# Fused attention and gated MLP: three edits to the opening, to slot 1 and to SyncE's queue

## The chip, the cores and the metric

The kernel runs on one NeuronCore of a Trainium2 chip. The metric is device time in microseconds (us), the median of several runs. A profile shows one further execution: its span runs from the first to the last instruction, and the execution's own time is a little longer than that.

## What is computed

The reference, cut to what matters (B = 8 batches, H = 8 heads, S = 576 rows, D = 64, 32 packed queries p per head; w_in is 512 x 2048, w_out 2048 x 512; all float32):

```python
def sm_attn(qq, kk, vv):
    s = scale * np.matmul(qq, kk.transpose(0, 1, 3, 2))
    a = np.exp(s - np.max(s, axis=-1, keepdims=True))
    a = a / (np.sum(a, axis=-1, keepdims=True) + 1e-09)
    return np.matmul(a, vv)

p_packed = sm_attn(p, k, v)
out = sm_attn(q, p_packed, p_packed)
x = out.transpose(0, 2, 1, 3).reshape(B * S, H * D)
h = x @ w_in
return (h * np.cos(h)) @ w_out
```

## The kernel before

The order of all work is written out by hand; nothing reorders it within an engine. The batches are worked off in slots. For batch b:

- k, q and v are cast to bf16 while POOL's DMA loads them (load, L92). kT and qT are their transposes. For the first batches TensorE makes them (pe_T, L103); later a DMA transpose does, issued in SyncE's queue (xbar, L96).
- s1 (L142): scores of the packed queries against kT, then their exponentials a1 on ScalarE. a1 is transposed to a1T, by TensorE (a1_pe, L163) or by a DMA transpose in SyncE's queue (a1_xbar, L158). pp (L173) multiplies a1T by v, pp_T transposes the result.
- ppw (L195) multiplies it by w_in, in four pieces of 512 columns; the result is PPW. s2, sums2 and normalise (L221 to L244) make the second softmax, a2n, from qT.
- The slot proper, slot(b) (L468): 16 steps, one for each 128 of the 2048 hidden columns. Each step runs h_mm (L248): four matmuls of PPW and a2n into a psA buffer, the cosine on ScalarE (L258), the product h * cos(h) on VectorE into gT (L261). There are three psA buffers in all, used in turn by all of these stages.
- Between these, TensorE is given output matmuls of the batch before (out_gen, L331; w_out, line L339): fill(n) issues the next n of them. 16 make a chunk of 128 rows, which ScalarE or VectorE copies to an osb buffer (there are four) and SyncE stores. In slot(s, hooks, keep, heavy) the output matmuls that are left, less keep, are spread over the 16 steps in proportion to the weights 1 + heavy[step]; a hook (other work given for a step) runs ahead of the step's output matmuls, but at a step that stands in heavy half of them go ahead of it.

Batch 0 has no earlier outputs to fill with, so the opening has matmuls of zeros in TensorE's order (warm, L373): 7 ahead of pack_p(0, 1), the transposes of the first packed queries, and 9 between it and pe_T of k0. Their operand wz is zeroed by VectorE (L388). Others stand later in the opening and aren't touched. q0's transposes, s2 and normalise follow, then 16 steps of h_one (L274) that alternate ScalarE and VectorE.

Slot 1 has as a hook at step 4 h_rest(0) (L286): the last 64 rows of batch 0 for all 16 column groups at once: 32 small matmuls into one psA buffer, one cosine over 1024 columns (L295), one product (L297, to joint). At step 5 comes a piece of ppw, at step 6 pack_p(2, 4), at steps 8 to 10 the transposes of k2.

In slots 3 to 7 (the loop at L542) SyncE's queue is given, in each slot that has a next one: xbar of q of the next batch (L551), a1_xbar of the next batch (L556), and, where there is one, xbar of k of the batch after (L559). SyncE's queue is in order, and the output stores stand in it as well. POOL waits for that k (the copy to gate, L560) before it issues the loads of v, q and k for later batches (L573).

Of the kernel before, what the change touches and what calls it, by code (L numbers as in the profile page):

```python
# [8 lines left out]
FP32 = mybir.dt.float32  # L9
# [6 lines left out]
def kernel(  # L16
# [10 lines left out]
    nc = tc.nc  # L27
# [12 lines left out]
    const = ctx.enter_context(tc.tile_pool(name="const", bufs=1))  # L40
# [22 lines left out]
    V, ACT, G = nc.vector, nc.scalar, nc.gpsimd  # L63
# [32 lines left out]
    def xbar(n, b):  # L96
        t = xT[n, b] = att_pool.tile([128, H * 3, TP], BF16, name=n + "T", tag=n + "T", bufs=2 if n == "k" else 1)
        nc.sync.dma_start_transpose(out=t, in_=bf[n, b].rearrange("p h x -> p (h x)"))
# [4 lines left out]
    def pe_T(n, b, engs=(V, V, V), groups=(0, 1, 2), own=None):  # L103
        if 0 in groups:
            xT[n, b] = att_pool.tile([128, H * 3, TP], BF16, name=n + "T", tag=n + "T", bufs=2 if n == "k" else 1)
        t = xT[n, b]
        flat = bf[n, b].rearrange("p h x -> p (h x)")
        for i in groups:
            ps = own(BF16) if own else psa(BF16)[:, 0, :]
            for j in range(8):  # L110
                o = 8 * i + j
                nc.tensor.transpose(ps[:, j * TP:(j + 1) * TP], flat[:, o * 128:(o + 1) * 128],  # L112
                                    ident[0:TP, 0:TP])
            copy(engs[i], t[:, 8 * i:8 * i + 8].rearrange("p a x -> p (a x)"),
                 ps[:, 0:8 * TP])

    def bank(dt=FP32):
        return O.tile([128, 512 if dt == FP32 else 1024], dt, name="ot", tag="ot")

    def pack_p(b0, b1, flat=None):  # L120
        ng = 2 * (b1 - b0)
        if flat is None:
            flat = psa(BF16).rearrange("p a x -> p (a x)")
        for g in range(ng):
            nc.tensor.transpose(flat[:, g * 128:(g + 1) * 128],
                                p_bf[:, 2 * b0 + g].rearrange("p t d -> p (t d)"), ident)
        V.tensor_copy(out=P2[:, b0:b1].rearrange("p b h n -> p (b h n)"), in_=flat[:, 0:ng * 128])
# [14 lines left out]
    def s1(b):  # L142
        ps = scores(lambda r, h, e: P2[r, b, h, :], xT["k", b])
        sm = small.tile([128, 2], FP32, name="sums1")
        for y in range(2):
            ACT.activation(  # L146
                out=a1[b % 2][:, y, :, 0:TP].rearrange("p (e m) x -> p e m x", e=2),
                in_=ps[y][:, :, 0:HS].rearrange("p e (m x) -> p e m x", m=3),
                func=AF.Exp, scale=scale, accum_out=sm[:, y:y + 1])
        sums1[b] = sm  # L150

    def recips(b):
        r1[b] = small.tile([128, 2], FP32, name="r1")
        rs1[b] = small.tile([128, 2], FP32, name="rs1")
        V.reciprocal(r1[b], sums1[b])
        V.tensor_scalar(out=rs1[b], in0=r1[b], scalar1=scale, scalar2=None, op0=ALU.mult)

    def a1_xbar(b):  # L158
        t = a1T[b] = att_pool.tile([128, 2, C, 128], BF16, name="a1T", tag="a1T")
        nc.sync.dma_start_transpose(out=t.rearrange("p a c x -> p (a c) x"),  # L160
                                    in_=a1[b % 2].rearrange("p a c x -> p (a c x)"))
# [33 lines left out]
    def ppw(b, n, eng=None, own=False, later=False, cuts=((0, 512),)):  # L195
        if b not in PPW:
            PPW[b] = ppw_pool.tile([128, 2, DF], BF16, name="PPW", tag="PPW")
        two = isinstance(eng, tuple)
        if own:
            ps = [bank(), bank()]  # L200
        else:
            t = psa()
            ps = [t[:, 0, :], t[:, 1, :]]
        for x in range(4):
            for y in range(2):
                r = slice(64 * y, 64 * y + 64)
                nc.tensor.matmul(ps[y][32 * x:32 * x + 32, :], ppT[b % 2][r, 0, x, :],  # L207
                                 w_in_bf[r, x, n * 512:(n + 1) * 512], start=True, stop=True)

        def evacuate(cuts=cuts):  # L210
            if own or two:
                for a, z in cuts:
                    for y in range(2):
                        copy(eng[y] if two else eng, PPW[b][:, y, n * 512 + a:n * 512 + z], ps[y][:, a:z])
            else:
                copy(eng or (V, ACT)[n % 2], PPW[b][:, :, n * 512:(n + 1) * 512], t)
        if later:
            return [lambda c=c: evacuate((c,)) for c in cuts]
        evacuate()

    def s2(b):  # L221
        a2u[b] = att_pool.tile([128, 2, S], BF16, name="a2u", tag="a2u")
        ps = scores(lambda r, h, e: ppT[b % 2][r, (h + e) % 2, h // 2, :], xT["q", b])
        for y in range(2):
            ACT.activation(out=a2u[b][:, y].rearrange("p (e x) -> p e x", e=2),  # L225
                           in_=ps[y][:, :, 0:HS], func=AF.Exp, scale=rs1[b][:, y:y + 1])

    def sums2(b, y):
        if b not in lns:
            lns[b] = att_pool.tile([128, 2, S], FP32, name="lns", tag="lns")  # L230
        ps = psa()
        for e in range(2):
            nc.tensor.matmul(ps[:, e, 0:HS], ones_blk, a2u[b][:, y, e * HS:(e + 1) * HS],  # L233
                             start=True, stop=True)
        ACT.activation(out=lns[b][:, y].rearrange("p (e x) -> p e x", e=2),  # L235
                       in_=ps[:, :, 0:HS], func=AF.Ln)

    def normalise(b):
        a2n[b] = a2n_pool.tile([128, 2, S], BF16, name="a2n", tag="a2n")
        for y in range(2):  # L240
            ACT.activation(out=lns[b][:, y], in_=lns[b][:, y], func=AF.Exp, scale=-1.0)  # L241
        for y in range(2):
            V.scalar_tensor_tensor(out=a2n[b][:, y], in0=a2u[b][:, y], scalar=r1[b][:, y:y + 1],  # L243
                                   in1=lns[b][:, y], op0=ALU.mult, op1=ALU.mult)  # L244
# [105 lines left out]
    def set_filler(b):  # L350
        fill(1000)
        filler[0] = out_gen(b)
        filler[1] = 16 * n_chunks(b)

    def fill(n):
        while n > 0 and filler[1] > 0:
            next(filler[0])
            filler[1] -= 1
            n -= 1
# [9 lines left out]
    def dup_p(a, b, eng):  # L369
        for t in range(2):  # L370
            eng.tensor_copy(out=p_bf[:, a:b, t, :], in_=p_raw[:, a:b, :])

    def warm(n, wps=None):  # L373
        wps = bank() if wps is None else wps
        for _ in range(n):
            nc.tensor.matmul(wps, wz[:, 0:128], wz, start=True, stop=True)  # L376

    nc.sync.dma_start(out=p_raw[:, 0:2, :], in_=p_rows[:, 0:2, :])
    load("k", 0)
# [6 lines left out]
        load_w_in(n)  # L386
    wz = const.tile([128, 512], BF16, name="wz")
    V.memset(wz, 0.0)  # L388
    ACT.preload_act_table_set(EXP_SET)
    V.memset(ones_blk, 0.0)  # L390
    for j in range(4):
        V.memset(ones_blk[j * 32:(j + 1) * 32, j * 32:(j + 1) * 32], 1.0)
    for t in a1:
        V.memset(t[:, :, :, TP:128], 0.0)

    warm(7)
    dup_p(0, 2, V)
    pack_p(0, 1)
    warm(9)
    pe_T("k", 0, (V, ACT, V))  # L400
    s1(0)
    load_w_in(3)
# [83 lines left out]
    def tk(n, b, i):  # L486
        return lambda: pe_T(n, b, (ACT, V, ACT), (i,))

    def cross(n, b):
        return lambda: xbar(n, b)  # L490
# [1 line left out]
    osb_eng[0] = ACT  # L492
    slot(1, [(2, lambda: ppw(1, 2, (ACT, V))), (4, lambda: h_rest(0)),
             (5, lambda: ppw(1, 3, (ACT, V))), (6, lambda: pack_p(2, 4)), (8, tk("k", 2, 0)), (9, tk("k", 2, 1)),
             (9, cross("q", 2)), (10, tk("k", 2, 2)), (12, cross("k", 3))], 4)
    ACT.preload_act_table_set(EXP_SET)
    osb_eng[0] = V
    G.tensor_copy(out=gate, in_=xT["k", 3][0:1, 0, 0:1])
# [43 lines left out]
    for s in range(3, B):  # L542
        nxt = s + 1 < B
        ACT.preload_act_table_set(EXP_SET)
        osb_eng[0] = V
        fill(1000)
        set_filler(s - 1)
        s2(s)
        ppw(s, 2, V)
        if nxt:  # L550
            xbar("q", s + 1)  # L551
        fill(8)
        if nxt:
            s1(s + 1)
            ppw(s, 3, V)
            a1_xbar(s + 1)  # L556
            recips(s + 1)
            if s + 2 < B:
                xbar("k", s + 2)  # L559
                G.tensor_copy(out=gate, in_=xT["k", s + 2][0:1, 0, 0:1])  # L560
        else:
            ppw(s, 3, V)
        fill(4)
        sums2(s, 0)
        fill(5)
        sums2(s, 1)
        normalise(s)
        ACT.preload_act_table_set(SIN_SET)
        fill(13)
        osb_eng[0] = ACT  # L570
        for n, b in (("v", s + 2), ("q", s + 2), ("k", s + 3)):
            if b < B:
                load(n, b)  # L573
        slot(s, [(5, lambda: pp(s + 1, ACT)), (6, lambda: pp_T(s + 1, ACT)), (10, lambda: pw2(s + 1))] if nxt else [], 5, {10: 3})
# [33 lines left out]
```

## Time and profile before

| | us |
|---|---|
| Median of 3 runs | 250.38 (250.29 to 250.45) |
| Profiled execution, its own time | 249.44 |
| Its span | 247.5 |
| TensorE busy | 238.6 |
| ScalarE busy | 170.6 |
| VectorE busy | 158.0 |
| Zero matmuls (L376) into ot, 32 of them, and 3 into psA | 11.4 busy for the 32 |

PE is TensorE's matmuls, PEld its weight loads, which overlap them; DVE is VectorE, ACT ScalarE, POOL GpSimd, SP SyncE, and a q behind an engine's name means its queue of DMA issues. L339 is line 339 of the kernel before. Ends of matmuls are modelled, so the distance from one start to the next tells more than a duration: a 128x512 bf16 matmul has a duration of 0.38 us in the page, and in a dense stretch the next one starts 0.216 us later. A row such as "4.36 3.48 PE L376 MATMUL ot<-wz ... x9" is a run of 9 instructions that started at 4.36 us and ended 3.48 us later; in brackets stands the idle time of the engine before it, and what ended it. The mean granted TensorE clock of the execution is 0.997.

### The profile page before, as it was taken

How to read it: one execution, taken by the hardware profiler on the slowest of the kernel's cores; microseconds unless marked ns; L12 is line 12 of the kernel's file. 1: busy time of each engine (PE TensorE's matmuls, PEld its weight loads, DVE VectorE, ACT ScalarE, POOL GpSimd, SP SyncE). 2: the span in 40 equal slices, each digit the busy share in tenths (PEclk: the TensorE clock that was granted, in tenths of full speed). 3: DMA queues.
4: the chain of work that ended last, by engine and by line, in shares of the span. 5: the costliest groups of instructions: out<-in, count | busy, mean ns of one | idle time of the engine just before them, and what ended most of it. 6: DMA issues, size and time to landing. Idle time of an engine off the chain costs nothing.

```text
span 247.5 us, 5472 instructions
## 1 busy us (share of the span) xinstructions
PE 238.6 (96%) x2247; PEld 128.4 (52%) x2247; DVE 158.0 (64%) x243; ACT 170.6 (69%) x284; POOL 38.1 (15%) x61
## 2 busy tenths in 40 slices
PE   8989989999999999999999999999999999999993
PEld 3553344566545554565446554565456554665452
DVE  3369976776549777578757666578756685774000
ACT  2369998767568777888787677978886685874110
POOL 8532420200400040004002200030000000000000
PEclk9999999999999999999999999999999999999998
DMA  6999999999699989997999995989371113111123
GB/s 88 204 210 208 203 206 230 200 230 194 132 210 166 218 147 212 215 202 118 215 230 197 165 209 97 176 162 185 89 161 45 42 45 84 43 33 55 52 75 85
DMA packets 63992, 37.37 MB, mean 151 GB/s; under 512 B 36592, under 2 KB 59376, under 8 KB 63968
## 3 DMA queue, kind: packets, MB, share of 16 engines
q0 software_dynamic: 23184, 18.81, 49.9%
q1 hardware_dynamic: 40624, 18.09, 35.1%
q8 instruction: 17, 0.28, 0.5%
q10 hardware_dynamic: 160, 0.13, 0.2%
q14 instruction: 7, 0.06, 0.1%
HBM read 37.22 MB, written 9.44 MB: 189 GB/s over the span
## 4 chain that ended last, share of the span: by engine, by line
PE 82%; ACT 4%; DVE 4%; issue 0%; DVEq 0%; ACTq 0%
PE ot L339 49%; PE psA L254 22%; PE psA L207 3%; PE psA L137 2%; PE ot L325 1%; PE psH L280 1%; PE psA L233 1%; PE psA L180 1%; DVE gT L284 1%; DVE PPW L87 1%; ACT a2u L225 1%; DVE gT L261 1%; ACT L446 1%; DVE joint L297 0%; PE psA L112 0%; ACT cosT L258 0%
## 5 line engine op out<-in xcount | busy, mean ns | idle before, releaser
L339 PE MATMUL ot<-w_out_bf,gT 128*128 128x512 bf16 x512 | 133.0, 380 | 0.0
L261 DVE TENSOR_TENSOR gT<-psA,cosT 128x576 bf16<-128x576 f32 x112 | 83.5, 757 | 33.5 <-ACT cosT L258 32.6
L258 ACT ACTIVATE cosT<-psA 128x576 bf16<-128x576 f32 x112 | 72.9, 653 | 26.8 <-PE psA L254 25.0
L254 PE MATMUL psA<-a2n,PPW 128*128 128x288 bf16 x448 | 73.2, 286 | 0.1
L339 PEld LDWEIGHTS <-gT 128*128 128x128 bf16 x512 | 47.2, 98 | 43.7 <-issue 7.8
L254 PEld LDWEIGHTS <-PPW 128*128 128x128 bf16 x448 | 43.8, 98 | 30.7 <-issue 1.3
L87 DVE CAST PPW<-psA 128x1024 bf16<-128x1024 f32 (+1 forms) x25 | 26.1, 1050 | 7.3 <-PE psA L207 7.3
L265 POOL COPY joint<-gT 128x512 bf16<-128x512 bf16 x14 | 8.6, 614 | 94.1 <-DVE gT L261 94.1
L87 DVE COPY osb<-ot 128x512 f32<-128x512 f32 (+1 forms) x14 | 9.4, 671 | 21.3 <-PE ot L325 17.4
L85 ACT COPY osb<-ot 128x512 f32<-128x512 f32 (+1 forms) x23 | 13.2, 575 | 13.7 <-PE ot L339 12.6
L243 DVE SCALAR_TENSOR_TENSOR a2n<-a2u,r,lns 128x576 bf16<-128x576 bf16 x16 | 12.4, 815 | 8.5 <-ACT lns L241 8.5
L146 ACT ACTIVATE a<-psA 128x576 bf16<-128x576 f32 x16 | 10.3, 647 | 8.3 <-PE psA L137 8.3
L235 ACT ACTIVATE lns<-psA 128x576 f32<-128x576 f32 x16 | 10.3, 651 | 6.5 <-PE psA L233 5.9
L339 PE MATMUL ot<-w_out_bf,joint 128*128 128x512 bf16 x48 | 12.8, 379 | 0.0
L376 PE MATMUL ot<-wz 128*128 128x512 bf16 x32 | 11.4, 486 | 1.3 <-DVE wz L388 1.2
L225 ACT ACTIVATE a2u<-psA,rs 128x576 bf16<-128x576 f32 x16 | 11.0, 737 | 1.5 <-PE psA L137 1.4
L207 PE MATMUL psA<-w_in_bf,ppT 64*32 64x512 bf16 x224 | 10.4, 380 | 0.1
L284 DVE TENSOR_TENSOR gT<-psH,cosT 128x512 bf16<-128x512 f32 x16 | 9.9, 682 | 0.4 <-ACT cosT L283 0.4
L241 ACT ACTIVATE lns<-lns 128x576 f32<-128x576 f32 x16 | 10.0, 674 | 0.0
L85 ACT CAST PPW<-psA 128x1024 bf16<-128x1024 f32 (+1 forms) x9 | 7.4, 822 | 2.8 <-PE psA L207 2.8
L283 ACT ACTIVATE cosT<-psH 128x512 bf16<-128x512 f32 x16 | 8.7, 619 | 0.7 <-DVE gT L284 0.4
L280 PE MATMUL psH<-a2n,PPW 128*128 128x512 bf16 x32 | 8.2, 381 | 0.7 <-DVE PPW L87 0.6
(88 smaller groups left out, 163.4 us busy)
## 6 DMA issues: line engine op xcount, KB each, us to landing
kbf<-in_k_dram POOLq DMA_DIRECT2D x8, 576.0 KB, 12.9
vbf<-in_v_dram POOLq DMA_DIRECT2D x8, 576.0 KB, 7.5
qbf<-in_q_dram POOLq DMA_DIRECT2D x8, 576.0 KB, 10.2
out_dram<-osb SPq DMA_DIRECT2D x24, 192.0 KB, 3.0
out_dram<-osb SPq DMA_DIRECT2D x22, 128.0 KB, 2.4
w_in_bf<-in_moe_w_in_dram POOLq DMA_DIRECT2D x4, 512.0 KB, 16.3
w_out_bf<-in_moe_w_out_dram POOLq DMA_DIRECT2D x4, 512.0 KB, 20.9
out_dram<-osb SPq DMA_DIRECT2D x26, 64.0 KB, 2.0
```

The costliest lines, as they stand in the source:

```text
L85: ACT.copy(out=out, in_=in_)
L87: eng.tensor_copy(out=out, in_=in_)
L207: nc.tensor.matmul(ps[y][32 * x:32 * x + 32, :], ppT[b % 2][r, 0, x, :], w_in_bf[r, x, n * 512:(n + 1) * 512], start=True, stop=True)
L225: ACT.activation(out=a2u[b][:, y].rearrange("p (e x) -> p e x", e=2), in_=ps[y][:, :, 0:HS], func=AF.Exp, scale=rs1[b][:, y:y + 1])
L243: V.scalar_tensor_tensor(out=a2n[b][:, y], in0=a2u[b][:, y], scalar=r1[b][:, y:y + 1], in1=lns[b][:, y], op0=ALU.mult, op1=ALU.mult)
L254: nc.tensor.matmul(ps[:, e, 0:HS], PPW[b][:, y, fc * 128:(fc + 1) * 128], a2n[b][:, y, e * HS:(e + 1) * HS], start=(y == 0), stop=(y == 1))
L258: ACT.activation(out=csv, in_=ps[:, :, 0:HS], func=AF.Sin, bias=PI_HALF)
L261: V.tensor_tensor(out=gT[b][:, fc, :].rearrange("p (e x) -> p e x", e=2), in0=ps[:, :, 0:HS], in1=csv, op=ALU.mult)
L280: nc.tensor.matmul(ps, PPW[b][:, y, fc * 128:(fc + 1) * 128], a2n[b][:, y, 0:512], start=(y == 0), stop=(y == 1))
L284: V.tensor_tensor(out=gT[b][:, fc, 0:512], in0=ps, in1=cs, op=ALU.mult)
L339: nc.tensor.matmul(pss[c], w, w_out_bf[:, fc, :], start=(fc == 0), stop=(fc == NFC - 1))
L376: nc.tensor.matmul(wps, wz[:, 0:128], wz, start=True, stop=True)
```

## The change

Three edits. The first seven zero matmuls become two with fp32 operands, and the nine behind pack_p become one with fp32 operands and three bf16 ones; the fp32 zeros are a new tile, wz4, which VectorE zeroes right behind wz. In the loop for slots 3 to 7, q's DMA transpose is issued behind a1's instead of ahead of it. In slot 1, step 4 gets a weight of 3 instead of 1 in the spreading of output matmuls. The 48 that are spread there went three to a step; they now go 2, 3, 3, 2, 8, 3, 3, 2, 3, 3, 2, 3, 3, 2, 3, 3, with four of the eight of step 4 ahead of h_rest.

```diff
-    def warm(n, wps=None):
-        wps = bank() if wps is None else wps
+    def warm(n, wps=None, w=None):
+        wps, w = bank() if wps is None else wps, wz if w is None else w
         for _ in range(n):
-            nc.tensor.matmul(wps, wz[:, 0:128], wz, start=True, stop=True)
+            nc.tensor.matmul(wps, w[:, 0:128], w, start=True, stop=True)
...
     wz = const.tile([128, 512], BF16, name="wz")
     V.memset(wz, 0.0)
+    wz4 = const.tile([128, 512], FP32, name="wz4")
+    V.memset(wz4, 0.0)
...
-    warm(7)
+    warm(2, None, wz4)
     dup_p(0, 2, V)
     pack_p(0, 1)
-    warm(9)
+    warm(1, None, wz4)
+    warm(3)
     pe_T("k", 0, (V, ACT, V))
...
-             (9, cross("q", 2)), (10, tk("k", 2, 2)), (12, cross("k", 3))], 4)
+             (9, cross("q", 2)), (10, tk("k", 2, 2)), (12, cross("k", 3))], 4, {4: 2})
...
         ppw(s, 2, V)
-        if nxt:
-            xbar("q", s + 1)
         fill(8)
         if nxt:
             s1(s + 1)
             ppw(s, 3, V)
             a1_xbar(s + 1)
+            xbar("q", s + 1)
             recips(s + 1)
```

## The prediction, made before the changed kernel had run

> **What bounds the kernel now.** I read the page first, then the chain of waits, then the timelines of the three places that the diff touches.
>
> ```profile
> PE 238.6 (96%) x2247; PEld 128.4 (52%) x2247; DVE 158.0 (64%) x243; ACT 170.6 (69%) x284; POOL 38.1 (15%) x61
> ...
> PE 82%; ACT 4%; DVE 4%; issue 0%; DVEq 0%; ACTq 0%
> ```
>
> TensorE is busy for 96% of the span and carries 82% of the chain that ended last. From 36 us on, the matmuls of L339 and L254 follow one another almost without a gap. A change off TensorE is worth something only where TensorE stands still, and a microsecond lost early is lost at the end. The opening is different, so I read it by its rows (start us, us, what).
>
> ```profile
> 1.19 3.17 PE L376 MATMUL ot<-wz 128*128 128x512 bf16 x7 [1.19 <-DVE wz L388]
> 4.15 0.42 PE L125 MATMUL psA<-ident,p_bf 128*128 128x128 bf16 x2
> 4.36 3.48 PE L376 MATMUL ot<-wz 128*128 128x512 bf16 x9
> 7.68 1.19 PE L112 MATMUL psA<-ident,kbf 96*128 96x96 bf16 x24
> ```
>
> ```profile
> 6.50 0.15 PEld L376 LDWEIGHTS <-wz 128*128 128x128 bf16 x1 [0.28 <-issue]
> 6.92 0.15 PEld L376 LDWEIGHTS <-wz 128*128 128x128 bf16 x1 [0.28 <-issue]
> 7.25 0.10 PEld L376 LDWEIGHTS <-wz 128*128 128x128 bf16 x1 [0.17 <-issue]
> 7.48 0.10 PEld L112 LDWEIGHTS <-kbf 96*128 96x128 bf16 x1
> ```
>
> The zero matmuls start 0.427 us apart (1.59, 2.02, ... 6.50, 6.92), then 0.327 once, then 0.216. So TensorE works at half speed until about 7.15 us, 5.96 us after its first matmul, though the page's clock row shows nothing of it. The check: 16 x 0.427 + 0.21 for the two transposes after 1.19 would end at 8.23 if all were slow. What lies behind 7.15 takes half, so the end is (8.23 + 7.15) / 2 = 7.69; the trace has 7.68.
>
> ```profile
> 1.30 0.89 POOL L94 DMA_DIRECT2D kbf<-in_k_dram  x1 [0.85 <-POOLq L592]
> ```
>
> ```profile
> kbf<-in_k_dram POOLq DMA_DIRECT2D x1, 576.0 KB, 6.1
> ```
>
> The first k load is issued at 1.30 and lands 6.1 us later, at 7.44. TensorE is thus at most 0.24 us behind the data when it takes up k0. The next gate is close too: q0 is issued at 3.48, lands 9.8 us later (13.32), and is transposed from 13.43.
>
> **Part 1, the zero matmuls.** Sixteen bf16 matmuls (16 x 0.427 us slow) become three with fp32 operands and three bf16. The fp32 zeros need a memset. The 256-word one took 0.27 us and a 64-word one 0.11, so 512 words take about 0.27 + 256 x 0.16 / 192 = 0.49 us. TensorE begins 0.46 later, at 1.65. The memsets queued behind on VectorE end at 2.70 instead of 2.24. The casts of p after them still wait for p, which lands at 2.75, so these 0.46 us are covered; if p came at once, the casts would be later by them, and still 2 us ahead of the transposes at about 5.
>
> No fp32 matmul stands in this trace; call its price at half speed P. The lower end is the nearest row, a bf16 matmul of the same shape: 0.427. For the upper end I take an estimate from rows: an fp32 operand is as wide as two bf16 ones, on both sides, so four half-products, each with the stream of 0.427 and a weight load of 0.15 (the slow PEld rows) that isn't hidden: 4 x 0.577 = 2.31. I take 4 x 0.427 = 1.71, because the weight loads in the rows above start under the running matmul. With the same switch at 7.15, k0 starts at (1.65 + 3P + 0.21 + 3 x 0.427 + 7.15) / 2 = 5.15 + 1.5 P. That is 7.71 for 1.71 (**+0.03 us**) and 8.61 for 2.31 (+0.93). For 0.427 the zeros end at 4.4 and TensorE idles until k0 lands: k0 starts at 7.48, but a lead stops at q0, which leaves 0.1 at most, and TensorE may still be slow.
>
> The Trainium skill, FP8 and Floating Point Precision, section "TensorE Precision Notes", counts four passes through the array for true fp32; by it the matmul is 1.71 as well. The rule that speaks against the change is in TensorE: Matmul & The Clock Gate, Part 1: the warm-up is a budget of time, about 3.4 us of sustained activity, and not a number of matmuls. By this page fewer matmuls buy nothing as such. Our row differs from its figure, with 5.96 us instead of 3.4; by 3.4 after 1.65 the switch would come at 5.05 and k0 would start at its landing, which makes the sum 0.1 us smaller (q0's landing stops the rest).
>
> Does a delay at k0 reach the end? k0's transposes feed s1, a1, pp and then q0's transposes, which start 0.11 us after q0's landing, so a delay isn't absorbed there. From 18.80 to 27.05 VectorE is the chain without a gap. The four pieces of w_in land at 19.42, 21.92, 24.46 and 27.22 and none is waited for longer than that chain. So a delay of k0 passes whole into the TensorE-bound rest.
>
> **Part 2, slot 1.** 48 output matmuls, three a step, become 2, 3, 3, 2, 8, 3, 3, 2, 3, 3, 2, 3, 3, 2, 3, 3. At step 4 four of the eight go ahead of h_rest, four behind it.
>
> ```profile
> 46.83 0.81 PE L339 MATMUL ot<-w_out_bf,gT 128*128 128x512 bf16 x3
> 47.48 0.65 PE L254 MATMUL psA<-a2n,PPW 128*128 128x288 bf16 x4
> 48.06 0.41 PE L207 MATMUL psA<-w_in_bf,ppT 64*32 64x512 bf16 x8
> 48.41 0.82 PE L339 MATMUL ot<-w_out_bf,gT 128*128 128x512 bf16 x3
> 49.37 0.65 PE L254 MATMUL psA<-a2n,PPW 128*128 128x288 bf16 x4
> ```
>
> ```profile
> 48.09 1.23 DVE L297 TENSOR_TENSOR joint<-psA,cosR 128x1024 bf16<-128x1024 f32 x1 [0.55 <-ACT cosR L295]
> ```
>
> Three output matmuls are 0.65 us of stream, so TensorE stands from 49.06 to 49.37: step 6 wants the psA buffer of h_rest, which VectorE frees at 49.32. One more matmul there fills 0.216 of these 0.31 us, and it is missing later, at steps (7, 10, 13) with nothing waiting: **-0.22 us**. Bounds: the first chunk's copy (ScalarE, 0.60) now goes ahead of step 5's cosine, which can hand the wait to pack_p at step 6, 0.08 us of gap now; then the gain is 0. With both gaps and the 0.09 ones ahead of the k2 transposes gone it would be 0.47.
>
> **Part 3, SyncE's queue, slots 3 to 6.** Its order q, a1, k becomes a1, q, k.
>
> ```profile
> 99.71 4.16 SPq L98 DMA_TRANSPOSE qT<-qbf  x1
> 103.96 1.47 SPq L160 DMA_TRANSPOSE a1T<-a  x1
> 105.54 3.43 SPq L98 DMA_TRANSPOSE kT<-kbf  x1
> ```
>
> In slot 3 the exponentials end at 99.89, so a1 can go at once and land at 103.9 instead of 107.9. q goes at 101.4 and lands near 107.7 instead of 106.06; k starts at 105.5 as before. In slots 4 to 6 q started before the exponentials ended (123.21, 151.77, 176.24 against 125.13, 153.47, 178.70), and now waits for them behind a1: q, k, and the output stores behind them move back by 1.9, 1.7 and 2.4 us. Cover: pp(4) starts at 108.56, 0.6 us after a1T lands, and isn't held by it; qT is used 13 to 21 us after landing (120.95 against 107.7 in slot 3; 202.87 against 186 in slot 6); kT at 151.71 against 136.0 and 176.94 against 164.2. POOL waits for kT ahead of the loads of v, q, k: they land 1.9 later (v at 143.2 for a use at 162.13, q at 146.8 ahead of 154.9). Joint copies behind these issues are used a slot later; the stores have four osb buffers. Cost **0**. Bounds: -0.6, as much as a1T's slack in slot 3 could be missing in another run, and +0.5, were one store late enough to hold an output copy (0.58).
>
> **The sum.** 247.5 + 0.03 - 0.22 + 0 = 247.3 us of span. Around the span lie 249.44 - 247.5 = 1.94. That profiled execution is 0.94 below the median of the runs shown, 250.38; I carry the difference over: 250.38 - 0.19 = **250.2 us**. What differs by less than 0.2%, 0.5 us, counts as no change.
>
> **Rivals.** (A) Unhidden weight loads: the fp32 matmul costs 2.31, k0 starts 0.93 late, less 0.22: 251.1, slower. It decides from P = 1.84 (+0.22, slower than before) and counts from P = 2.17. For it: the fp32 matmuls have no weight load of their own in the built order, so nothing shows that one is pulled ahead. Against: in the bf16 rows all are. (B) The switch to full speed doesn't come at 7.15, because the fp32 zeros keep TensorE less busy than the sixteen did. All zeros slow end at 8.28 (+0.59). The 24 transposes of k0 take 0.08 each (the slow 128-wide one took 0.107) instead of 1.15 us together: +0.77. The 16 matmuls of s1 add some 0.3. Less 0.22 this gives 251.8. For it: the switch took 5.96 us of dense work, and the new zeros start later. Against: 12 half-products and three bf16 are as much slow time. (C) Faster: k0 starts at its landing (0.1) and slot 1 gains all 0.47: 249.8. (D) The reordering bites: a store or load 2 us later finds a reader; 250.7. Nothing in the rows above comes within 2 us.
>
> **How the numbers follow.** Forecast 0.38, A 0.18, B 0.18, C 0.24, D 0.02 (just inside no change). Faster 0.24, no change 0.40, slower 0.36. The forecast's own range is 249.9 to 250.6 (the ends of slot 1 and P up to 2.0). C reaches to 249.6 with part 3's lower end in it; A and B to 251.8. I take 249.6 to 251.8.
>
> **What would show it.** In the new profile: fp32 rows 1.7 us apart; k0's transposes at 7.7 (A: 8.6; B: zeros 0.427 apart to the end, and k0's transposes over 1.2 us long); h6 in slot 1 less than 0.15 us after its last output matmul; a1T landing 4 us earlier in slot 3 and pp(4) still held by VectorE. The prediction is wrong if k0 starts outside 7.4 to 8.0, or if pp, s2 or s1 in slots 3 to 6 wait for a transpose.

## The result, and the profile after

| | us |
|---|---|
| Before, median of 12 runs | 250.46 (250.24 to 254.87) |
| After, median of 12 runs | 249.73 (249.35 to 250.08) |
| Ratio of the paired runs | 0.9957 (0.9941 to 0.9973) |
| Profiled execution after, its own time | 249.53 |
| Its span | 247.6 |

The changed kernel is faster by 0.73 us in the median. No change, 250.2, was forecast as likeliest. The two profiles, however, show no gain: the span is 247.6 after and 247.5 before. That contradiction is the subject of what follows. Line numbers of the changed kernel are 2 to 3 higher around the zero matmuls (L390 is wz's memset).

The page of after, engines and chain of waits:

```profile
PE 234.0 (95%) x2204; PEld 128.3 (52%) x2240; DVE 158.5 (64%) x244; ACT 170.3 (69%) x284; POOL 38.2 (15%) x61
...
PE 82%; DMA 6%; DVE 4%; ACT 3%; issue 2%; POOL 2%; DVEq 0%; ACTq 0%; POOLq 0%
```

TensorE still carries 82% of the chain. New in it is DMA with 6%: the load of w_in, for which TensorE waits at one place in the opening. Off that chain, TensorE now takes up k0 when its load lands (7.58). TensorE's timeline of after (start, us, what, idle before):

```profile
1.73 3.78 PE L376 MATMUL ot<-wz 128*128 128x512 f32 x4 [1.73 <-DVE wz L390]
5.31 0.42 PE L125 MATMUL psA<-ident,p_bf 128*128 128x128 bf16 x2
5.52 2.22 PE L376 MATMUL ot<-wz 128*128 128x512 f32 x5
7.62 1.19 PE L112 MATMUL psA<-ident,kbf 96*128 96x96 bf16 x24
...
16.68 0.50 PE L112 MATMUL ot<-ident,kbf 96*128 96x96 bf16 x8
...
19.76 0.41 PE L207 MATMUL ot<-w_in_bf,ppT 64*32 64x512 bf16 x8 [0.36 <-DMA w_in_bf<-in_moe_w_in_dram]
```

An fp32 matmul is two rows here ("f32 x4" ahead of pack_p is two matmuls; "x5" is one of them and the three bf16 ones). Ahead of the transposes at 5.31 there are four rows, which start at 1.73, 2.75, 3.60 and 4.46. Behind the first, which takes 1.02, the starts are 0.853 us apart, so one fp32 matmul costs 1.71. k0 is taken up at 7.62 and k1 at 16.68, before it was 7.68 and 16.64. Then ppw waits for w_in, which landed at 19.72 and not at 19.42: the whole stretch is 0.30 late from here.

Slot 1, TensorE and VectorE of after:

```profile
48.43 0.65 PE L254 MATMUL psA<-a2n,PPW 128*128 128x288 bf16 x4
49.01 0.41 PE L207 MATMUL psA<-w_in_bf,ppT 64*32 64x512 bf16 x8
49.58 0.59 PE L339 MATMUL ot<-w_out_bf,gT 128*128 128x512 bf16 x2 [0.16 <-issue]
50.10 0.65 PE L254 MATMUL psA<-a2n,PPW 128*128 128x288 bf16 x4
```

```profile
48.82 1.23 DVE L297 TENSOR_TENSOR joint<-psA,cosR 128x1024 bf16<-128x1024 f32 x1 [1.41 <-ACT cosR L295]
```

The product to joint ends at 50.05 and step 6 starts at 50.10, still at VectorE's hand. (The x2 of L339 lacks a record; the 0.16 ahead of it is its third matmul.) But three output matmuls more have gone ahead of step 6, two of them ahead of h_rest and one in the gap behind it, and the 0.30 of delay is 0.08 from here on: slot 1 gives back 0.22. The rest of the execution adds nothing, and 0.08 is the difference of the spans.

So the pair of profiles agrees with the sum of the prediction to 0.3 us, and the medians don't agree with the pair. The 12 runs of after lie around its profiled execution (249.35 to 250.08, against 249.53). Those of before don't: 249.44 was profiled, and the lowest of the 12 is 250.24. Of the 35 runs of before in each of three later sessions the lowest are 249.87, 249.96 and 249.50. The profile of before that everything was read from is an execution that hardly occurs. What was lucky in it?

### The profile page after: what moved, and what is told of

The parts are those of the page before. It is cut to its first block, busy times and chain, and to the rows that moved or that the text cites. A ratio compares the mean times of both kernels' runs of the same rounds, so it can differ in the third digit from the quotient of the medians.

```text
span 247.6 us, 5423 instructions
## 1 busy us (share of the span) xinstructions
PE 234.0 (95%) x2204; PEld 128.3 (52%) x2240; DVE 158.5 (64%) x244; ACT 170.3 (69%) x284; POOL 38.2 (15%) x61
## 4 chain that ended last, share of the span: by engine, by line
PE 82%; DMA 6%; DVE 4%; ACT 3%; issue 2%; POOL 2%; DVEq 0%; ACTq 0%; POOLq 0%
PE ot L339 48%; PE psA L254 22%; DMA w_in_bf<-in_moe_w_in_dram 6%; PE psA L207 3%; PE psA L137 2%; PE ot L325 1%; PE psA L233 1%; PE psA L180 1%; DVE gT L284 1%; PE psH L280 1%; DVE PPW L87 1%; ACT a2u L225 1%; DVE gT L261 1%; POOL kbf L94 1%; ACT L449 1%
## 5 line engine op out<-in xcount | busy, mean ns | idle before, releaser
L339 PE MATMUL ot<-w_out_bf,gT 128*128 128x512 bf16 x482 | 128.2, 379 | 2.8 <-issue 1.9
L339 PEld LDWEIGHTS <-gT 128*128 128x128 bf16 x512 | 47.3, 98 | 43.5 <-issue 7.8
L339 PE MATMUL ot<-w_out_bf,joint 128*128 128x512 bf16 x47 | 12.6, 379 | 0.1
L376 PE MATMUL ot<-wz 128*128 128x512 bf16 (+1 forms) x23 | 10.2, 548 | 2.0 <-DVE wz L390 1.7
```

The source lines that it names most:

```text
L339: nc.tensor.matmul(pss[c], w, w_out_bf[:, fc, :], start=(fc == 0), stop=(fc == NFC - 1))
```

## The experiments

Twelve kernels ran, in three sessions of four, each kernel 11 or 12 times and each session with 35 runs of the kernel before on the same chip. Medians of different sessions are compared with care: the changed kernel itself has 249.73 in the result and 249.35 in e5. Medians in us:

| kernel | zeros | slot 1 | queue | median (range) | before beside it | ratio (95%) |
|---|---|---|---|---|---|---|
| e1_zeros | new | old | old | 250.49 (249.54 to 251.99) | 250.42 | 0.9993 (0.9959 to 1.0026) |
| e2_slot1 | old | new | old | 250.31 (250.12 to 251.51) | 250.42 | 0.9979 (0.9950 to 1.0008) |
| e3_queue | old | old | new | 250.45 (249.60 to 251.33) | 250.42 | 0.9980 (0.9952 to 1.0007) |
| e4_before | old | old | old | 250.43 (249.86 to 251.14) | 250.42 | 0.9988 (0.9960 to 1.0015) |
| e5_after | new | new | new | 249.35 (249.23 to 250.34) | 250.34 | 0.9972 (0.9961 to 0.9982) |
| e6_no_queue | new | new | old | 250.37 (249.29 to 255.05) | 250.34 | 0.9991 (0.9959 to 1.0023) |
| e7_pad | padded | new | new | 250.00 (249.62 to 250.33) | 250.34 | 0.9974 (0.9950 to 0.9998) |
| e8_sums_first | new, and an order | new | new | 249.92 (249.29 to 251.87) | 250.34 | 0.9979 (0.9951 to 1.0007) |
| e9_no_zeros | old | new | new | 250.06 (249.93 to 251.19) | 250.31 | 0.9989 (0.9975 to 1.0002) |
| e10_no_slot1 | new | old | new | 249.69 (249.33 to 250.64) | 250.31 | 0.9976 (0.9961 to 0.9991) |
| e11_later_fetch | fewer still | new | new | 250.03 (249.29 to 250.58) | 250.31 | 0.9980 (0.9966 to 0.9993) |
| e12_later_no_queue | fewer still | new | old | 250.37 (249.26 to 251.62) | 250.31 | 1.0002 (0.9983 to 1.0020) |

By the medians, no part alone is worth more than 0.11; zeros with slot 1 (e6) are worth nothing, slot 1 with the queue (e9) 0.25, zeros with the queue (e10) 0.62, all three 0.99. The ratios alone separate these cases poorly, since their intervals overlap, and the traces have to say why they differ.

### Each part by itself, and the kernel before again

At this point the main theory was that the zeros made the gain through the clock, and that slot 1 added its 0.22.

e1_zeros: of the diff only warm, wz4 and the two places that call it with wz4.

> The fp32 zeros alone. Theory 1 (in most executions of the kernel before TensorE comes to full speed later than the 7.15 us of its one profile, and with the fp32 zeros it does not): about -0.5 us against before, ratio 0.998, and k0's transposes from 7.5 to 7.8 us. Theory 2 (the gain is SyncE's new order) and theory 3 (the gain is slot 1): within 0.1 us of before.

e2_slot1: of the diff only the weight.

```diff
-             (9, cross("q", 2)), (10, tk("k", 2, 2)), (12, cross("k", 3))], 4)
+             (9, cross("q", 2)), (10, tk("k", 2, 2)), (12, cross("k", 3))], 4, {4: 2})
```

> The new spread of slot 1's output matmuls alone. Theories 1 and 2: -0.22 us, the 0.216 us matmul that fills the gap ahead of step 6, ratio 0.999. Theory 3: -0.7 us, the whole gain.

e3_queue: of the diff only the order a1, q, k.

```diff
-        if nxt:
-            xbar("q", s + 1)
...
+            xbar("q", s + 1)
```

> SyncE's new order alone. Theories 1 and 3: 0 within 0.1 us, pp of slots 3 to 6 held by VectorE or nothing, as before. Theory 2 (in most executions a1's transpose lands after pp could start, unlike in the one profile): -0.5 us.

e4_before: the kernel before, no edit.

> The kernel before once more, unchanged, for the scatter of its executions and a second profile. All theories: ratio 1.000. Theory 1: spans from 247.5 to 249 us, most of them over 248, and a profile of a longer execution shows zeros 0.427 us apart to a later time than 7.15 and the difference in time already there at k0's scores. Theory 2: the opening is the same in every profile and the difference begins at a pp of slots 3 to 6.

e1 gave nothing where some half a microsecond was expected: a miss for the clock theory. By itself it doesn't refute it, since a gain of the opening can be lost again further on, as will be seen. e2 gave 0.11 in the median and e3 nothing. e4 brought the clue. Its span is 248.5, 1.0 more than that of before although it is the same kernel, and 0.9 of it arises at one place. TensorE's timeline of before and then of e4:

```profile
16.39 0.40 PE L233 MATMUL psA<-a2u,ones_blk 128*128 128x288 bf16 x2
16.64 0.50 PE L112 MATMUL ot<-ident,kbf 96*128 96x96 bf16 x8
```

```profile
16.36 0.40 PE L233 MATMUL psA<-a2u,ones_blk 128*128 128x288 bf16 x2
17.55 0.51 PE L112 MATMUL ot<-ident,kbf 96*128 96x96 bf16 x8 [0.78 <-DMA kbf<-in_k_dram]
```

The second k load, k1, landed at 16.32 in the one and at 17.50 in the other. A load adds 1 to its semaphore from each of the 16 DMA engines, and TensorE waits for all of them. In e4 fifteen were there by 16.30, and the sixteenth came 1.20 later. What kept that one engine busy is in the DMA view of e4, in the stretch 15.3 to 15.4:

```profile
q0 software_dynamic: 24, 0.02, 116.0%
q8 instruction: 1, 0.02, 58.4%
```

One packet of 16 KB in queue 8, which carries instructions, started at 15.34 and took 0.94 us; a packet of k1 takes 0.08. The Trainium skill, Runtime: NRT & Kernel Launch, section "Instruction fetch mechanics", says that a sequencer refills its instruction memory in blocks of 16 KiB over a DMA queue of its own, and that the cost is mostly hidden. The packet agrees (17 of them make 0.28 MB on the profile's page). The last part doesn't hold here: the cost falls on a load.

From the traces of all fourteen profiles (us):

| | k0 taken up | fetch | k1's 15th | k1's 16th | 16th after the fetch's end | a1T of batch 4 landed | pp(4) starts | span |
|---|---|---|---|---|---|---|---|---|
| before | 7.68 | 15.69 to 16.65 | 16.18 | 16.32 | -0.33 | 107.92 | 108.56 | 247.5 |
| after | 7.62 | 15.82 to 16.80 | 16.34 | 16.42 | -0.38 | 107.23 | 108.64 | 247.6 |
| e1_zeros | 7.35 | 15.64 to 16.61 | 16.16 | 17.66 | 1.05 | 109.78 | 109.83 | 248.7 |
| e2_slot1 | 8.00 | 16.50 to 17.45 | 16.79 | 16.81 | -0.64 | 110.48 | 110.53 | 249.4 |
| e3_queue | 7.48 | 15.37 to 16.33 | 16.28 | 17.44 | 1.11 | 107.64 | 110.34 | 249.3 |
| e4_before | 7.49 | 15.34 to 16.27 | 16.30 | 17.50 | 1.23 | 106.92 | 109.48 | 248.5 |
| e5_after | 7.36 | 15.58 to 16.53 | 16.12 | 16.16 | -0.37 | 106.61 | 108.39 | 247.3 |
| e6_no_queue | 7.59 | 15.58 to 16.55 | 16.39 | 17.70 | 1.15 | 109.35 | 109.44 | 248.4 |
| e7_pad | 7.80 | 15.53 to 16.48 | 16.60 | 17.56 | 1.09 | 106.76 | 109.31 | 248.3 |
| e8_sums_first | 7.61 | 15.96 to 16.92 | 16.41 | 17.99 | 1.07 | 110.99 | 111.04 | 249.9 |
| e9_no_zeros | 7.58 | 15.36 to 16.31 | 16.39 | 17.40 | 1.09 | 105.26 | 109.15 | 248.1 |
| e10_no_slot1 | 7.43 | 15.82 to 16.79 | 16.20 | 16.23 | -0.56 | 106.06 | 108.68 | 247.7 |
| e11_later_fetch | 8.14 | 16.12 to 17.07 | 16.10 | 16.25 | -0.82 | 106.72 | 108.79 | 247.8 |
| e12_later_no_queue | 8.15 | 16.18 to 17.15 | 16.10 | 16.15 | -1.00 | 109.49 | 109.53 | 248.4 |

The profiles fall into two classes and nothing lies between. Either all 16 parts of k1 are in before the fetch ends, and the sixteenth comes within 0.15 of the fifteenth; or the sixteenth comes 1.05 to 1.23 after the end of the fetch. In e4 and e6 the last packets of k1 start as the fetch ends (the first at 16.25 and 16.54, against its ends at 16.27 and 16.55): they had stood behind it on its engine. The sixteen packets of 4 bytes that follow k1's data, one for each part, say the same in all fourteen: in the seven late profiles the last of them starts between 0.02 ahead of the fetch's end and 0.43 behind it, in the seven early ones at least 0.66 ahead of it. That is the first race, between an instruction fetch and the last sixteenth of a load, and it is worth about 0.9 us.

e2 shows a second race. k1 is early there (16.81), but the span is 249.4. SyncE's queue and TensorE's timeline of e2 in slot 3:

```profile
102.72 3.74 SPq L98 DMA_TRANSPOSE qT<-qbf  x1
106.55 1.47 SPq L160 DMA_TRANSPOSE a1T<-a  x1
```

```profile
110.53 0.55 PE L180 MATMUL psA<-vbf,a1T 96*32 96x64 bf16 x48 [1.73 <-DMA a1T<-a]
```

q4's load landed at 102.67, 3.01 later than in the profile of before. Its transpose waits for it, a1's stands behind that one, and pp(4) waits 1.73. In the profile of before a1T landed 0.64 ahead of pp(4). This execution of e2, 251.26, is one of the three of its twelve that lie above 250.5. After the change the queue reads:

```profile
100.01 2.61 SPq L160 DMA_TRANSPOSE a1T<-a  x1
102.72 4.43 SPq L98 DMA_TRANSPOSE qT<-qbf  x1
107.25 3.22 SPq L98 DMA_TRANSPOSE kT<-kbf  x1
```

q4's load was as late there (102.53), and pp(4) didn't wait: a1T landed at 107.23 and pp(4) began at 108.64.

The theory from here on (F): the zeros change how many instructions lie ahead, and so when the fetch starts; the new order takes the late q4 out of the way; the gain is there when both races are won. In e1 to e4 a late or early k1 can't be read as the effect of a part, as one profile shows one draw. Against it stood the clock (C): the fp32 zeros bring k0 forward or full speed sooner.

### The fetch or the clock; the queue with the zeros

e5_after: the changed kernel again, no edit.

> The changed kernel again, beside the next three on one chip. Theory F (two races: TensorE's 16 KB instruction fetch against the last packets of the second k load in the opening, and a1's transpose against pp in slot 3; the zeros help the first, the queue order the second): about -0.7 us against before, k1 landed by 16.9 us. Theory C (the zeros bring the clock earlier): the same figure, so this run is the yardstick for the others.

e6_no_queue: the changed kernel with the old order of SyncE's queue.

```diff
         ppw(s, 2, V)
+        if nxt:
+            xbar("q", s + 1)
...
             a1_xbar(s + 1)
-            xbar("q", s + 1)
```

> Zeros and slot 1 without the new queue order. Theory F: in executions in which slot 3's q lands after 101 us, pp of slot 3 is held 1 to 1.8 us by a1's transpose; the median 0.3 to 1 us above the changed kernel, with a wide scatter. Theory C and the prediction as it stood (queue order worth 0): the same as the changed kernel within 0.15 us.

e7_pad: the instructions that the fp32 zeros had saved are put back as 11 narrow zero matmuls, behind the fp32 ones.

```diff
     warm(1, None, wz4)
-    warm(3)
+    wps = bank()
+    for _ in range(11):
+        nc.tensor.matmul(wps[:, 0:128], wz[:, 0:128], wz[:, 0:128], start=True, stop=True)
```

> The changed kernel with its three bf16 zero matmuls of 512 columns cut into eleven of 128: the same TensorE time (11 x 0.056 against 3 x 0.216 us), 16 more instructions. Theory F: the fetch starts again right behind the scores of s2, 0.3 to 0.5 us earlier, and the second k load lands after 17.3 us in many executions: median 0.3 to 0.9 us above the changed kernel. Theory C: the fp32 zeros are all there, so the same as the changed kernel.

e8_sums_first: the sums ahead of the transposes of p, without the zero matmul between them, to move the fetch further back.

```diff
-    pack_p(1, 2, bank(BF16))
-    warm(1)
     sums2(0, 0)
+    pack_p(1, 2, bank(BF16))
```

> The changed kernel with sums2(0, 0) ahead of pack_p(1, 2) and without the one zero matmul between them: the instruction at which the fetch starts now waits for ScalarE. Theory F: the fetch starts after 16.2 us, the second k load lands by 16.9 in every profile, median equal to the changed kernel or up to 0.3 us below it (the pack costs about 0.1). Theory C: no reason for a gain; 0.1 us slower.

e5: eight of eleven runs are at 249.23 to 249.49 and three at 250.21 to 250.34, two clusters 0.9 apart, as the table's two classes of k1 are. That they are these classes is inferred: only the run at 249.23 was profiled. e7 keeps the fp32 zeros, the new slot 1 and the new queue, and loses 0.65 of it: no run of its eleven is below 249.62. TensorE in e5 and then in e7:

```profile
15.64 0.29 PE L125 MATMUL ot<-ident,p_bf 128*128 128x128 bf16 x2
...
16.48 0.50 PE L112 MATMUL ot<-ident,kbf 96*128 96x96 bf16 x8
```

```profile
16.03 0.28 PE L125 MATMUL ot<-ident,p_bf 128*128 128x128 bf16 x2
...
17.61 0.51 PE L112 MATMUL ot<-ident,kbf 96*128 96x96 bf16 x8 [0.57 <-DMA kbf<-in_k_dram]
```

e7 is 0.39 later than e5 at the transposes of p, yet its fetch is 0.05 earlier in time (15.53 against 15.58): counted from the transposes of p, 0.50 ahead of them and not 0.06. The padding moved the fetch in the program's order, as F asks. (The other fifteen parts of k1 also came 0.48 later in e7, which by itself makes the race harder to win in this one draw.) The 0.39 themselves come from k0's load, which landed at 7.76 and was taken up at 7.80 (e5: 7.31 and 7.36), so they are not the zeros' doing; TensorE was through with them in both before k0 was there. C falls by that, and by e1 and e5: k0 is taken up at 7.35 and 7.36 there, and the spans are 248.7 and 247.3. Nor did the fp32 zeros bring full speed sooner: by the starts of the rows TensorE left half speed at 4.8 (e8) to 7.7 us (e11, e12) with them, and at 3.9 (e3) to 7.15 (before) with the bf16 ones. What e7's times show is weaker in the ratios than in the runs: the ratios are 0.9974 and 0.9972 and their intervals overlap, while eight of e5's eleven runs lie below every run of e7.

e6 has the zeros and slot 1 and loses everything, 1.02 against e5 in the median. Its profile lost the first race, so it doesn't show the second one; e12 does, below. e8 missed: the fetch came at 15.96 and still caught k1 (16.41, then 17.99), and a1T, though issued ahead of q, landed at 110.99, held pp(4) 0.6, and no gain over e5 came out.

### Slot 1 and the zeros taken out, and a later fetch

e9_no_zeros and e10_no_slot1: the changed kernel with the old zeros, and with the old weight in slot 1; the diffs are those parts of the change, undone.

> Slot 1 and queue order, with the old bf16 zeros. Theory F (the opening's race between instruction fetch and second k load, and slot 3's race between a1's transpose and pp): the second k load lands after 17.3 us in nearly every execution, as in the kernel before, and slot 1 gives its 0.2: median 250.0 to 250.2, few executions above 250.7. Rival A (the parts simply add up as measured alone, 0 and -0.1): 250.3.

> Zeros and queue order, with the old spread in slot 1. Theory F: two groups, about 249.5 (k1 landed by 16.9 us) and 250.4 (after 17.3), more in the lower one; the median 0.2 above the changed kernel's, 249.6. Rival A: 250.35, the zeros and the queue being worth nothing.

e11_later_fetch: at two places one fp32 zero matmul of 384 columns stands for three bf16 ones, and two more bf16 ones are dropped, so that still fewer instructions lie ahead of the fetch (warm takes the number of columns as a fourth argument).

```diff
     warm(1, None, wz4)
-    warm(3)
+    warm(1, None, wz4, 384)
     pe_T("k", 0, (V, ACT, V))
...
-    warm(3)
+    warm(1, None, wz4, 384)
     a1_pe(0)
-    warm(2)
+    warm(1)
     recips(0)
     pp(0)
-    warm(1)
```

> The changed kernel with eight TensorE instructions fewer ahead of q0 (fp32 zeros of 384 columns for the sets of three bf16 ones, one zero matmul fewer at two places). Theory F: the fetch starts later still, after 16.0 us; the second k load lands by 16.9 us in more executions than with the changed kernel; median 249.2 to 249.4 and fewer executions near 250.3. If the clock matters more: TensorE slower after k0, 0.3 us or more above the changed kernel.

e12_later_no_queue: e11 with the old order of SyncE's queue, as in e6.

> The kernel of e11 with the old order q, a1, k in SyncE's queue. Theory F: the second k load lands early, so TensorE reaches pp of slot 3 about 0.9 us sooner, and a1's transpose, still behind q's, holds it: what the opening gained is given back there, median 0.5 to 1.2 us above e11, with a profile in which pp of slot 3 waits for a1T. Rival A and the prediction as it stood: the same as e11.

e9 loses the gain of the zeros: ten of twelve runs are at 249.93 to 250.29, and its profile has the late k1. e10 keeps it: nine of twelve are at 249.33 to 249.91, three at 250.41 to 250.64. Its distance to e5 is 0.34 in the medians, of two sessions, but the ratios of the two (0.9976 and 0.9972) overlap; slot 1's 0.22 is seen in the rows and not separated by the times. In e11 the fetch and k1 came as wanted (16.12 and 16.25), but k0, landed at 7.39, was taken up at 8.14 only, because TensorE stayed at half speed there until about 7.7, in after only until 6.5 (the 384 fp32 columns themselves, 2 x 0.64 us at half speed, take as long as the three bf16 matmuls that they stand for, 3 x 0.427). q0's transposes began 0.63 behind q0's landing, and the gain went there. The median, 0.3 us and more above the changed kernel, is what was expected for the case that the clock matters more: a miss as a version. It doesn't confirm that fewer instructions start the fetch later either. Counted from the last of s2's matmuls the fetch starts at 0.26 in e11 and 0.31 in e12, no later than in e5 (0.34); it came late in time because TensorE itself was 0.62 late. What the pair does show is that k1 lands early where the fetch starts after 16.1.

e11 and e12 are the clean pair for SyncE's order, since both have k1 early. TensorE at pp(4) in e11 and in e12:

```profile
108.79 0.55 PE L180 MATMUL psA<-vbf,a1T 96*32 96x64 bf16 x48
```

```profile
109.53 0.56 PE L180 MATMUL psA<-vbf,a1T 96*32 96x64 bf16 x48 [0.70 <-DMA a1T<-a]
```

q4's load landed at the same time in both (100.72 and 100.57). In the old order a1T landed at 109.49, in the new one at 106.72, and of that difference 0.70 reaches TensorE and 0.6 the span; in the medians it is 0.34, less than expected.

This is why the parts don't add up. With k1 late TensorE comes to pp(4) at 109.15 to 109.48 where nothing else is late (e4, e7, e9), and the old order costs little there: pp(4) isn't held in e6, and by 0.15 in e1. With k1 early it comes at 108.4 to 108.8, and then the old order takes 0.70 (e12) or 1.73 (e2) of the gain away. The new order alone saves nothing, because TensorE is late anyway. None of the twelve is faster than the changed kernel beyond its intervals.

## Why the prediction was wrong, point by point

The step that failed is in the sum: "That profiled execution is 0.94 below the median of the runs shown, 250.38; I carry the difference over". That difference was taken for a constant around the kernel. It was mostly the price of the first race, which this execution had won: e4, the same kernel at 250.47 and so a typical execution, lost that race alone (its a1T landed 2.56 ahead of pp(4)), and its span is 1.0 longer. The second race costs little as long as the first is lost, and has to be won as well when the first is. With the change the profiled execution is 0.20 below its own median (249.53 and 249.73). The term therefore moved by -0.74, and the rows by +0.09 (249.53 - 249.44), which makes -0.65 against the median then shown. The change improved the chance of an execution that the profile of before showed as if it were the rule. The numbers to see it stood in the table: runs of 250.29 to 250.45, and a profile of 249.44, outside.

- Part 1, TensorE time: right. "P" was taken as 1.71 and is 2 x 0.853 = 1.71; k0 was put at 7.71 and came at 7.62. That this is so near is in part luck: k0's load landed at 7.58, 0.14 later than before, just as the zeros ended. Weight loads were not added to it, so rival A fell; k0's transposes take 1.19 as before, so B fell.
- Part 1, "With the same switch at 7.15": the half-speed rows end at about 6.5 in after, and in the profiles of bf16 zeros the switch lies anywhere between 3.9 (e3) and 7.15 (before). In e3, e4, e9 and e2 TensorE idles and takes up k0 0.04 to 0.05 behind its landing (7.44 to 7.95). The number 5.96 us was one draw too; in after it mattered little, in e11 and e12, where half speed lasted until 7.7, it made k0 0.75 and 0.87 late.
- Part 1, what else the edit moves: missing. It was priced by TensorE's time alone. That fewer instructions lie ahead of a fetch isn't in it, and putting them back costs 0.65 in the median between e5 and e7. That their number is what starts the fetch is inferred: no view shows what starts it.
- "none is waited for longer than that chain", of the four pieces of w_in: wrong in the profile of after, by 0.36 us of wait and 0.30 of delay. In before ppw followed w_in's landing by 0.04; this was no slack.
- Part 2: right, -0.22 in the rows, by the mechanism named, and VectorE still ends the wait, as said. That the first chunk's copy hands the wait on didn't happen.
- Part 3, "Cost 0": right for the one profile, wrong for the median. Its lower bound, "-0.6, as much as a1T's slack could be missing in another run", was the right thought: the slack is missing by 0.70 in e12 and 1.73 in e2. It was kept as a bound where it should have been weighed with a chance. The landing was wrong: a1T was put at 103.9, 4 us earlier, and came at 107.23, because it took 7.2 us from its issue against 4.0 in before; k's transpose, put at 105.5, was issued at 107.25. Why a1T took longer is open. On the other side nothing bit: moving q behind a1 delayed no reader, so rival D fell.
- Rival C, "faster", 249.8, is right in size (249.73), but by luck: the races aren't in it. Of its reasons, k0 near its landing is nearly right and worth 0.06; slot 1's full 0.47 is not, it was 0.22.

What stays open: which of the 16 engines carries the fetch, and why the same start, 15.58 in e5 and e6, catches k1 in one and misses it in the other (the race there is decided by how far that engine is with its sixteenth, which the trace doesn't give by engine). The start of the fetch also scatters within one kernel. Counted from the last of s2's matmuls it is -0.13 to 0.06 in e3, e4, e7 and e9, but 0.29 in before and 0.67 in e2; with the instructions saved it is 0.16 to 0.54 (after, e1, e5, e6, e8, e10), and 0.26 and 0.31 with still fewer (e11, e12). So the saving seems to shift the odds and doesn't decide a run. Why q4's load lands anywhere from 98.5 to 106.0 wasn't followed up.

## What to carry to other kernels

Compare the profiled execution's own time with the spread of the runs before reading anything from its rows: if it lies outside, its waits are not those of the median, and a second profile of the same kernel is worth more than a closer look at the first. A load lands with the last of its 16 engines, so list the increments of a load that is waited for, and look for what else ran on the missing engine. When two waits stand in a row, parts of a change that remove one each can be worth nothing alone and 0.7 to 1.0 us together.

## What the runs showed of the hardware that was not expected

- The opening's instruction fetch of 16 KB takes 0.94 to 0.98 us on a DMA engine, twelve times a data packet of k1 (0.079), and the load whose last share stands behind it lands 1.05 to 1.23 after the fetch's end, even where no data packet of it is left to start. In e1 the last data packet began at 15.80, the last 4-byte packet at 16.60, as the fetch ended at 16.61, and the sixteenth part counted at 17.66. From the last 4-byte packet to the count it takes 0.7 to 1.1 in the late profiles and 0.30 to 0.34 in the early ones; why isn't known.
- An fp32 128x512 matmul is issued as two rows of 0.853 us at half speed, four times the bf16 one (0.427) in all, with no weight load added.
- After the wait for k1 TensorE can fall back to half speed. In e3 it waited 0.78 us, and its timeline goes on with such rows:

```profile
18.55 1.49 PE L112 MATMUL ot<-ident,kbf 96*128 96x96 bf16 x16
```

The same 16 transposes take 1.02 in after. e8 shows the same 1.49, after a wait of 1.09. e4 waited as long as e3 and kept its speed, so the wait alone doesn't decide it. The granted clock in the stretch 17.6 to 20.9 is 0.50 in e3 and 1.00 in e4, and over the whole execution 0.993 in e3 and e8, where no other of the fourteen profiles is below 0.996.
